# A build-time ordering that learns of a shared SBUF port: Nyström attention and two feed-forward layers on one core

## Chip, core and metric

The kernel runs on one core of one Trainium2 chip. The metric is the device time of one execution in microseconds (us), the median over runs.

## What is computed

The reference runs three stages one after another, all in float32. Cut to what matters:

```python
# attention: 4 batches, 8 heads, 576 tokens, head width 64, 32 landmarks
q_lm = q.reshape(B, H, 32, 18, D).mean(axis=3)      # landmark means: sums of 18 rows
k_lm = k.reshape(B, H, 32, 18, D).mean(axis=3)
A, Bm, C = sm(q, k_lm), sm(q_lm, k_lm), sm(q_lm, k)  # softmax, scale 1/8
Z = Bm.T / (norm_1 * norm_inf + 1e-6)
for _ in range(6):
    Z = 2 * Z - Z @ Bm @ Z
x = A @ Z @ C @ v                                    # then (2304, 512)
h = x @ w_in                                         # 512 -> 2048
x = (h * tanh(softplus(h))) @ w_out                  # 2048 -> 512
h = x @ moe2_w_in
out = (h * sigmoid(h)) @ moe2_w_out
```

## The kernel before

**The work.** Attention is done in eight groups, each of one batch and four heads (class `Group`). For a group the keys `kn` and queries `qn` come in, `sums` (line 739) forms the landmark sums `lmk` and `lmq`, `transposed` (763) turns keys and queries, `main` (801) forms the 32 by 32 middle matrix, `c_side` (931) and `a_side` (998) the two outer softmaxes, and `newton` (901) the six iterations. A group leaves a 64 by 128 block `ut` of a small matrix and its softmax `at`.

`projection` (523) multiplies a batch's `ut` with 512 columns of the first layer's input weights `wa`, which gives `wp`; it is called "the first projection" below for batch 0 and columns 0 to 511, "the second" for batch 0 and the next 512. From then on the layers run in units: a unit of phase 0 or 1 is a pair of products for 288 tokens and 128 hidden columns, `emit_h` (573), then the activation `z` on ScalarE (ACT), its rounded copy and remainder `g` (`gated`, 592), and `emit_o` (610). Phase 0 takes the first half of the hidden columns of the first layer, and stores its sums to DRAM in `yh`; phase 1 takes the second half and adds what `partial` (636) reads back from `yh`; phase 2 is the second layer. Each product is made of three passes with numbers split in a rounded part and a remainder. Weights are stored as 64-bit numbers; `decode` (421) turns them into float32 on ACT and VectorE (DVE, tile `m` or `wa`) and splits them with a copy and a subtraction.

**The order.** The order of all instructions is set while the program is built, by `Line`: a table of how long each engine takes (`cost`), when each tile was last written or read (`depend`), and when each engine comes free. A step of the program that is due goes next on its engine; an operation that two engines can do goes to the one that `issue` (163) expects to end first: landmark sums to VectorE or GpSimd (POOL) (line 744), copies to ACT or VectorE, subtractions to VectorE or GpSimd. On the chip each engine then runs its list in that order and waits on semaphores. The estimate has therefore no part in the run; it only decides which instruction stands where, and on which engine.

**Padding.** While groups are unfinished, the loop writes two transposes of the identity matrix, with no use for their result, wherever TensorE is free by the estimate and has done little lately:

```python
            if not grown and line.cold():
                for ring in (y_r, h_r, t_r):
                    if ring.idle(line.now):
                        b_ = ring.take([128, 512], FP32)
                        for i in range(2):
                            T.transpose(out=b_[0][:, i * 128:i * 128 + 128], in_=ident, identity=ident)
```

In lists and rows they read `y<-ident`, `h<-ident` or `t<-ident`. They are instructions like others: TensorE does them in their place in the list. All instructions of `issue` have one line in a profile (193 before), so rows are told apart by tile names. PE is TensorE, PEld its weight loads, SP the engine that issues all transfers.

Of the kernel before, what the change touches and what calls it, by code (L numbers as in the profile page):

```python
# [52 lines left out]
def width(ap):  # L53
    return ap.size() // ap.shape[0]


class Line:
# [12 lines left out]
    def __init__(self, nc):  # L70
        self.nc = {"V": nc.vector, "A": nc.scalar, "P": nc.gpsimd, "T": nc.tensor}
        self.free = dict.fromkeys(["V", "A", "P", "T", "D", "W"], 0.0)
        self.now = 0.0
        self.free["D"] = 0.45
        self.end = 0.0
        self.last = set()
        self.past = collections.deque()
        self.busy, self.seen = {}, {}
        self.chains = []
        self.small = False  # L80
        self.count = itertools.count()

    def cost(self, e, name, kw):
        src = kw.get("in_", kw.get("in0"))
        n = width(src if name == "tensor_reduce" else kw["out"])
        psum = src is not None and src.space == bass.MemoryType.PSUM
        more = 0.0
        if e == "T":
            tiled = kw["out"].shape[0] < 96 and "lhsT" in kw
            if tiled and (kw["out"].start_partition() or kw["lhsT"].start_partition()):  # L90
                return 0.027 * self.clock()
            n *= self.clock() * self.columns(kw)
        elif e == "A":
            more = -0.04 if psum else 0.0
            more += 0.14 if "accum_out" in kw else 0.09 if kw.get("func") == ACTF.Ln else 0.0
        elif e == "P" and name == "tensor_scalar":
            n *= 0.46
        elif e == "V" and name in ("copy", "tensor_copy", "tensor_scalar", "scaled"):
            if not psum:
                n *= 0.5  # L100
            elif n < 300:
                n += 50
            more = 0.06 if hasattr(kw.get("scalar1"), "space") else 0.0
        elif e == "V" and name == "reciprocal" and n > 1:
            more = 0.09
        return self.FIXED[e] + more + n * self.EACH[e]

    @staticmethod
# [48 lines left out]
    def lately(self):  # L157
# [2 lines left out]
            self.past.popleft()  # L160
        return sum(x[1] for x in self.past)

    def issue(self, engines, name, kw, bias=0.0):
        def start(e):
            return max(self.now, self.free[e], self.depend(e, name, kw))

        e = min(engines, key=lambda e: start(e) + self.cost(e, name, kw) + (bias if e == "V" else 0.0))
        at = start(e)
        if e == "T":
            small = kw["out"].shape[0] < 96  # L170
            if self.small and not small:
                at = max(at, self.free["T"] + 0.055)
            self.small = small
        end = at + self.cost(e, name, kw)
        if e == "T":
            tick = int(at / self.WINDOW)
            rows = kw["lhsT" if "lhsT" in kw else "in_"].shape[0]
            part = rows * kw["out"].shape[0] / 16384 * self.columns(kw)
            self.past.append((at, width(kw["out"]) * part))
            self.busy[tick] = self.busy.get(tick, 0) + width(kw["out"]) * part  # L180
        self.free[e] = end
        self.end = max(self.end, end)
        self.last.add(e)
        self.record(e, kw, end)
        if name == "copy" and e != "A":
            name = "tensor_copy"
        if name == "scaled":
            k = dict(out=kw["out"], in_=kw["in_"])
            if e == "A":
                name, kw = "activation", dict(k, func=ACTF.Copy, scale=kw["scalar1"])  # L190
            else:
                name, kw = "tensor_scalar", dict(out=kw["out"], in0=kw["in_"], scalar1=kw["scalar1"], scalar2=None, op0=ALU.mult)
        r = getattr(self.nc[e], name)(**kw)  # L193
        return r
# [57 lines left out]
class Ring:  # L252
# [11 lines left out]
    def any(self):  # L264
        return any(p[1] for p in self.pools)
# [37 lines left out]
def kernel(  # L303
# [29 lines left out]
    NB = {0: 2 * B, 1: 2 * B, 2: -(-NT // 512)}  # L333
# [3 lines left out]
    def tokens(ph, t):  # L337
        return (t * SH, SH) if ph < 2 else (t * 512, min(512, NT - t * 512))
# [3 lines left out]
    V, A, P, T = (On(line, e) for e in "VAPT")  # L342
# [48 lines left out]
    def until(cond):  # L391
        while not cond():
            yield "W"

    def marked(*m):
        return lambda: all(a in marks for a in m)
# [239 lines left out]
    def partial(t):  # L636

        yp_t[t] = []
        n0, n = tokens(1, t)
        for d in range(KD):  # L640
            yield from until(lambda: ysb_r.any() and stored.get(("part", 0, t), LATE) <= line.now)
            yp_t[t].append(ysb_r.take([128, 512], FP32))
            line.transfer(nc.sync, out=yp_t[t][d][0][:, :n], in_=yh[d * 128:(d + 1) * 128, n0:n0 + n])
            yield "W"
# [456 lines left out]
    while todo or flight:  # L1101
# [52 lines left out]
        if hs:  # L1154
            line.add(gated(ph, t, f), "G", "A", line.free["T"] + 0.17 + SLACK)
            if first and ph == 1:
                line.add(partial(t), "C")
            if ph < 2 and t % 2 and f % 4 == 3:
                Ring.give(wp_t[t // 2, f // 4])
            if ph == 2 and last:  # L1160
                for x in x_t[t]:
                    Ring.give(x)
        else:
            Ring.give(g_t.pop((ph, t, f)))
            if ph < 2 and t == NB[ph] - 1:
                marks.add(("last", f))
# [33 lines left out]
```

## Time and profile before

| | |
|---|---|
| median of 3 runs | 891.68 us (890.7 to 892.5) |
| the profiled execution | 885.96 us |
| its span, first to last instruction | 884.1 us |
| busy: PE | 842.2 us (95%) |
| busy: PEld | 710.9 us (80%) |
| busy: DVE | 330.6 us (37%) |
| busy: ACT | 369.4 us (42%) |
| busy: POOL | 314.0 us (36%) |

The span is the time between the first and the last instruction of the profiled execution; its own time is 1.86 us longer. Busy shares are averages over the whole span. VectorE has next to nothing to do in the last third, so its share says little of the first.

### The profile page before, as it was taken

The numbers are of one execution on the slowest core, as the hardware profiler recorded it, in microseconds if no ns is written. First come the engines' busy times: TensorE is split into PE (matmuls) and PEld (weight loads), VectorE is DVE, ScalarE is ACT, GpSimd is POOL, SyncE is SP. The second block draws the span as 40 slices with busy tenths as digits, with TensorE's granted clock in tenths as the row PEclk, the third lists the DMA queues.
The fourth block names the chain that finished last, engine by engine and source line by source line (L and its number), as shares of the span: only waits on it lengthen the run. The fifth ranks groups of instructions, "written<-read, shape, count | busy, mean of one in ns | idle before, by whom it ended". The sixth has DMA issues, their size and how long they took to land.

```text
span 884.1 us, 14991 instructions
## 1 busy us (share of the span) xinstructions
PE 842.2 (95%) x5974; PEld 710.9 (80%) x5974; DVE 330.6 (37%) x618; ACT 369.4 (42%) x784; POOL 314.0 (36%) x310
## 2 busy tenths in 40 slices
PE   7789898989999999999999998999999999999996
PEld 5566576768989888999998886788888888888895
DVE  7989664544686572120108888300000000000000
ACT  4475666663555452433325444421232123212321
POOL 1343353222446372523326645521232123212221
PEclk9999999999999999999999999999999999999999
DMA  9665424100542531322226820020002000100100
GB/s 235 177 200 153 151 64 111 43 19 12 194 145 77 183 89 54 91 73 92 69 86 233 304 96 1 14 82 0 1 17 68 0 1 25 36 0 1 29 20 25
DMA packets 41861, 72.27 MB, mean 82 GB/s; under 512 B 5184, under 2 KB 29248, under 8 KB 41792
## 3 DMA queue, kind: packets, MB, share of 16 engines
q1 hardware_dynamic: 41792, 71.32, 26.7%
q8 instruction: 47, 0.77, 0.4%
q14 instruction: 22, 0.18, 0.1%
HBM read 57.15 MB, written 14.16 MB: 81 GB/s over the span
## 4 chain that ended last, share of the span: by engine, by line
PE 70%; DVE 13%; ACT 6%; DMA 5%; issue 3%; SPq 2%; POOL 0%; DVEq 0%; ACTq 0%; POOLq 0%
PE y L193 38%; PE h L193 28%; DVE m L193 7%; PE t L193 5%; DMA wst<-in_moe_w_out_dram 2%; ACT L193 2%; SPq L204 2%; DVE wa L193 1%; ACT z L193 1%; DMA kn<-in_k_dram 1%; ACT m L193 1%; DMA wst<-in_moe_w_in_dram 1%; ACT g L193 1%; DMA wp<-in_q_dram 1%; DVE lmk L193 1%
## 5 line engine op out<-in xcount | busy, mean ns | idle before, releaser
L193 POOL TENSOR_TENSOR g<-z,g 128x288 fp32r<-128x288 f32 (+2 forms) x196 | 198.8, 1021 | 379.8 <-ACT g L193 320.1
L193 PE MATMUL y<-g,wo 128*128 128x288 f32 x1536 | 229.2, 300 | 0.3 <-ACT ysb L193 0.3
L193 PEld LDWEIGHTS y<-g,wo 128*128 128x128 f32 x1536 | 209.2, 188 | 14.4 <-issue 10.8
L193 ACT ACTIVATE z<-h 128x288 f32<-128x288 f32 (+2 forms) x208 | 96.2, 468 | 284.7 <-PE h L193 252.5
L193 PE MATMUL h<-x,wi 128*128 128x512 f32 (+1 forms) x960 | 205.8, 371 | 2.6 <-DVE wi L193 1.8
L193 PE MATMUL y<-wo,g 128*128 128x512 f32 x864 | 203.1, 392 | 0.6 <-POOL g L193 0.6
L193 PEld LDWEIGHTS h<-x,wi 128*128 128x128 f32 x960 | 167.6, 188 | 36.9 <-DVE wi L193 1.7
L193 PEld LDWEIGHTS y<-wo,g 128*128 128x128 f32 x864 | 161.8, 188 | 36.6 <-POOL g L193 1.0
L193 PE MATMUL h<-at,wp 128*128 128x288 f32 x768 | 122.1, 303 | 9.7 <-ACT z L193 9.5
L193 PEld LDWEIGHTS h<-at,wp 128*128 128x128 f32 x768 | 107.0, 189 | 21.9 <-ACT z L193 13.1
L193 ACT CAST g<-z 128x288 fp32r<-128x288 f32 (+2 forms) x199 | 96.0, 491 | 21.7 <-PE y L193 18.0
L193 DVE SCALAR_TENSOR_TENSOR m<-wst,m 128x512 int32<-128x512 int32 x96 | 97.3, 1014 | 2.7
L193 DVE TENSOR_TENSOR x<-xst,x 128x512 fp32r<-128x512 f32 (+1 forms) x4 | 4.3, 1066 | 181.5 <-ACT x L193 181.4
L193 POOL TENSOR_TENSOR wo<-m,wo 128x512 fp32r<-128x512 f32 x29 | 39.5, 1363 | 59.5 <-ACT wo L193 41.0
L193 DVE TENSOR_SCALAR m<-m 128x512 int32<-128x512 int32 x48 | 33.2, 692 | 26.3 <-ACT m L193 26.2
L193 DVE TENSOR_TENSOR wp<-t,wp 128x512 fp32r<-128x512 f32 x32 | 20.6, 685 | 43.5 <-ACT wp L193 43.5
L193 DVE TENSOR_TENSOR ysb<-y,ysb 128x288 f32<-128x288 f32 x32 | 13.2, 458 | 60.1 <-PE y L193 60.1
L193 ACT ACTIVATE m<-wst 128x512 f32<-128x512 f32 x48 | 31.8, 669 | 1.6 <-DMA wst<-in_moe_w_out_dram 1.1
L193 POOL TENSOR_TENSOR x<-xst,x 128x512 fp32r<-128x512 f32 (+1 forms) x16 | 19.3, 1209 | 33.7 <-ACT x L193 33.7
L193 ACT ACT_TABLE_LOAD x23 | 29.5, 1283 | 2.8 <-PE h L193 1.7
L193 ACT CAST wp<-t 128x512 fp32r<-128x512 f32 x29 | 15.6, 589 | 32.2 <-PE t L193 32.2
L193 ACT CAST wo<-m 128x512 fp32r<-128x512 f32 x20 | 12.4, 620 | 33.6 <-DVE m L193 33.6
(158 smaller groups left out, 573.5 us busy)
## 6 DMA issues: line engine op xcount, KB each, us to landing
wst<-in_moe_w_out_dram SPq DMA_DIRECT2D x32, 512.0 KB, 7.4
wst<-in_moe_w_in_dram SPq DMA_DIRECT2D x28, 512.0 KB, 6.3
kn<-in_k_dram SPq DMA_DIRECT2D x32, 144.0 KB, 7.4
vn<-in_v_dram SPq DMA_DIRECT2D x8, 576.0 KB, 6.8
yh<-ysb SPq DMA_DIRECT2D x32, 144.0 KB, 1.8
ysb<-yh SPq DMA_DIRECT2D x32, 144.0 KB, 2.3
ys<-ysb SPq DMA_DIRECT2D x32, 144.0 KB, 2.2
out_dram<-ysb SPq DMA_DIRECT2D x72, 64.0 KB, 1.7
```

The costliest lines, as they stand in the source:

```text
L193: r = getattr(self.nc[e], name)(**kw)
L204: return engine.dma_start(**kw)
```

## The change

Three things change. `cost` adds 0.9 us to a long reduction on VectorE, which are the landmark sums. [...] And `partial` waits until all of phase 0's sums are on their way to DRAM before it takes buffers.

```diff
@@ __init__
+        self.held = {"V": collections.deque(), "P": collections.deque()}
@@ cost
+        elif e == "V" and name == "tensor_reduce" and n > 1000:
+            more = 0.9
@@ new functions of Line
+    @staticmethod
+    def holds(e, name, kw):
+
+        if e == "P":
+            return True
+        src = [kw[k] for k in ("in_", "in0", "in1") if k in kw]
+        if e != "V" or any(x.space == bass.MemoryType.PSUM for x in src):
+            return False
+        return len(src) > 1 or name in ("copy", "tensor_copy", "tensor_scalar", "scaled")
+
+    def alone(self, e, at, name, kw):
+
+        if self.holds(e, name, kw):
+            for a, b in self.held["P" if e == "V" else "V"]:
+                if a < at + 0.05 and b > at:
+                    at = max(at, b)
+        return at
@@ issue
         def start(e):
-            return max(self.now, self.free[e], self.depend(e, name, kw))
+            at = max(self.now, self.free[e], self.depend(e, name, kw))
+            return self.alone(e, at, name, kw)
...
+        if self.holds(e, name, kw):
+            self.held[e].append((at, end))
+            while len(self.held[e]) > 24:
+                self.held[e].popleft()
@@ partial
+        yield from until(marked(("part", 0, NB[0] - 1)))
```

No operation is computed differently. What changes is the order, the engine of those operations that have a choice, and the padding. Over the whole program the lists differ in these counts:

| | before | now |
|---|---|---|
| padding transposes on TensorE | 214 | 312 |
| of them ahead of the first projection | 88 | 142 |
| of them ahead of the second projection | 190 | 264 |
| landmark sums on VectorE / on GpSimd | 10 / 6 | 8 / 8 |
| copies of `wo` and `wi` on VectorE / on ACT | 18 / 30 | 4 / 44 |
| subtractions of `wo` and `wi` on VectorE / on GpSimd | 8 / 40 | 1 / 47 |
| subtractions of `g` on VectorE / on GpSimd | 12 / 180 | 1 / 191 |
| table loads on ACT | 23 | 29 |

The three places below are those that the prediction speaks of. Instructions have line 193 before and 219 now.

TensorE, the third to the sixth iteration of `newton` for the first group (`t<-yu`; `h<-yu` is the second group's), before:

```order
L193 MATMUL t<-yu 32x96 x4
L193 MATMUL y<-ident 128x128 x8
L193 MATMUL h<-yu 32x96 x4
L193 MATMUL t<-yu 32x96 x4
L193 MATMUL y<-ident 128x128 x4
L193 MATMUL h<-yu 32x96 x4
L193 MATMUL t<-yu 32x96 x4
L193 MATMUL y<-ident 128x128 x4
L193 MATMUL h<-yu 32x96 x4
L193 MATMUL y<-ident 128x128 x4
L193 MATMUL t<-yu 32x64 x4
```

and now:

```order
L219 MATMUL t<-yu 32x96 x4
L219 MATMUL y<-ident 128x128 x16
L219 MATMUL h<-yu 32x96 x4
L219 MATMUL t<-yu 32x96 x4
L219 MATMUL y<-ident 128x128 x8
L219 MATMUL h<-yu 32x96 x4
L219 MATMUL t<-yu 32x96 x4
L219 MATMUL y<-ident 128x128 x6
L219 MATMUL h<-yu 32x96 x4
L219 MATMUL t<-yu 32x64 x4
```

Between the same iterations stand 30 padding transposes where there were 20.

TensorE around the first projection (`t<-wa,ut`), before:

```order
L193 MATMUL y<-ident 128x128 x4
L193 MATMUL t<-wa,ut_136 32x512 x8
L193 MATMUL y<-ident 128x128 x14
L193 MATMUL t<-lmT 32x32 x4
L193 MATMUL y<-ident 128x128 x6
L193 MATMUL h<-at_656,wp 128x288 x2
L193 MATMUL t<-Tk,lmT 32x288 x8
L193 MATMUL h<-at_656,wp 128x288 x16
```

and now:

```order
L219 MATMUL t<-lmT 32x32 x4
L219 MATMUL y<-ident 128x128 x10
L219 MATMUL t<-wa,ut_136 32x512 x8
L219 MATMUL y<-ident 128x128 x22
L219 MATMUL t<-Tk,lmT 32x288 x8
L219 MATMUL h<-at_632,wp 128x288 x18
```

The third group's small product `t<-lmT` moved ahead of the projection, its scores `t<-Tk,lmT` ahead of the first unit's products, and the padding behind the projection grew from 20 to 22 and that ahead of it from 4 to 10.

ACT, from the small softmax `eb` to the softmax `ec` of the sixth group, with the activations `z` and copies `g` of units between them, before:

```order
L193 ACT_TABLE_LOAD
L193 ACTIVATE eb,sbm<-t,nmb 128x32
L193 COPY ut_138<-t 64x128
L193 ACTIVATE bn<-eb,rb 128x32
L193 ACTIVATE ec,sc_2249<-t,nmc 128x288 x2
```

and now:

```order
L219 ACT_TABLE_LOAD
L219 ACTIVATE eb,sbm<-t,nmb 128x32
L219 CAST g<-z 128x288
L219 ACT_TABLE_LOAD
L219 ACTIVATE z<-h 128x288
L219 CAST g<-z 128x288
L219 ACTIVATE z<-h 128x288
L219 CAST at_2456<-a_t 128x576
L219 CAST g<-z 128x288
L219 ACT_TABLE_LOAD
L219 ACTIVATE ec,sc_2496<-t,nmc 128x288 x2
```

Between a group's two exponentials now stand activations of units, and with them two more table loads.

## Rows read from the trace of the kernel before

**Rows 1.** Stretches: length; busy us of PE, PEld, DVE, ACT, POOL; clock, DMA share, GB/s.

```profile
0.00:20.00 20.00, 14.87 (x141) 10.98 (x141) 13.45 (x33) 9.00 (x25) 1.52 (x13) 1.00 0.95 236
20.00:44.70 24.70, 19.08 (x313) 13.68 (x312) 24.60 (x64) 12.32 (x31) 9.51 (x9) 1.00 0.69 182
44.70:92.60 47.90, 43.79 (x525) 31.18 (x524) 43.34 (x105) 30.98 (x70) 18.72 (x19) 1.00 0.60 176
...
98.10:217.60 119.50, 109.39 (x1204) 86.06 (x1198) 59.56 (x168) 72.03 (x153) 39.92 (x47) 0.99 0.19 52
217.60:600.00 382.40, 372.77 (x2453) 336.08 (x2453) 182.76 (x231) 166.70 (x364) 170.93 (x158) 1.00 0.34 109
600.00:884.10 284.10, 276.83 (x1298) 230.29 (x1296) 2.02 (x2) 74.98 (x138) 72.11 (x64) 0.99 0.07 17
```

**Rows 2.** PE's waits, 20 to 100 us: total us, times, longest.

```profile
PE t L193 <- DVE yu L193: 4.7, 8, 1.1
PE t L193 <- ACT Tk L193: 2.0, 2, 1.6
PE h L193 <- DVE yu L193: 1.0, 1, 1.0
```

**Rows 3.** PE's waits, 100 to 215 us.

```profile
PE h L193 <- ACT z L193: 3.5, 4, 1.2
PE t L193 <- ACT ec L193: 3.0, 2, 1.9
PE t L193 <- ACT Tk L193: 1.3, 1, 1.3
```

**Rows 4.** PE's waits, 215 to 600 us.

```profile
PE h L193 <- ACT z L193: 6.0, 7, 1.2
```

**Rows 5.** Order of time on PE around padding: start us, us, operation.

```profile
45.88 1.75 PE L193 MATMUL y<-ident 128*128 128x128 f32 x14
47.56 0.27 PE L193 MATMUL t<-lmT 64*32 64x32 f32 x8
...
74.14 2.36 PE L193 MATMUL h<-ident 128*128 128x128 f32 x18
76.51 0.37 PE L193 MATMUL t<-yu 32*32 32x96 f32 x8
```

**Rows 6.** Order of time, all engines, 21 us: one VectorE shift beside GpSimd.

```profile
21.19 1.16 POOL L193 TENSOR_TENSOR at<-at,am 128x576 f32<-128x576 f32 x1 [18.84 <-DVE rc L193]
...
21.48 1.15 DVE L193 TENSOR_SCALAR wa<-wa 128x512 int32<-128x512 int32 x1
```

**Rows 7.** Tile wa, all its instructions: duration ns min/median/max.

```profile
L193 DVE TENSOR_SCALAR wa<-wa x16: 355/424/1295, 21.5 to 264.3; 128x512 int32<-128x512 int32 x16
```

**Rows 8.** Groups of instructions, 0 to 215 us: count, busy us, mean ns, idle before.

```profile
L193 DVE TENSOR_REDUCE lmk<-kn 128x64 f32<-128x1152 f32 x5 | 10.9, 2188 | 5.7 <-DMA kn<-in_k_dram 5.7
L193 DVE TENSOR_REDUCE lmq<-wp 128x64 f32<-128x1152 f32 x1 | 2.2, 2160 | 0.1
L193 POOL TENSOR_TENSOR t<-kn 128x576 f32<-128x576 f32 x3 | 4.9, 1642 | 0.0
L193 DVE CAST wo<-m 128x512 fp32r<-128x512 f32 x3 | 2.4, 790 | 0.0
L193 DVE TENSOR_TENSOR g<-z,g 128x288 fp32r<-128x288 f32 x5 | 3.4, 684 | 2.5 <-ACT g L193 1.9 <-POOL at L193 0.6
```

**Rows 9.** ACT's table loads, 0 to 215 us: count, busy us, mean ns.

```profile
L193 ACT ACT_TABLE_LOAD x22 | 28.2, 1283 | 2.8 <-PE h L193 1.7 <-PEq L1184 0.7
```

**Rows 10.** Order of time on ACT from 145 us.

```profile
145.33 1.28 ACT L193 ACT_TABLE_LOAD   x1
146.63 0.41 ACT L193 ACTIVATE z<-h 128x288 f32<-128x288 f32 x1
```

**Rows 11.** The same columns as rows 1, 100 to 120 us.

```profile
100.00:120.00 20.00, 16.66 (x190) 12.96 (x189) 11.69 (x23) 12.88 (x26) 8.36 (x10) 0.91 0.01 4
```

**Rows 12.** The page's costliest groups: the addition of the stored half product.

```profile
L193 DVE TENSOR_TENSOR ysb<-y,ysb 128x288 f32<-128x288 f32 x32 | 13.2, 458 | 60.1 <-PE y L193 60.1
```

## Prediction

> **What bounds the kernel now.** I began with busy time by stretch [rows 1], because the averages over the span hide the stages. From 600 us on TensorE is busy 276.8 of 284.1 us with the second layer's products, and from 217.6 to 600 us 372.8 of 382.4. The work there is fixed, so the change can win only what TensorE idles: 9.6 us in the middle. Before 217.6 us the eight groups run. VectorE is busy 24.6 of 24.7 us up to the first projection (44.7 us) and 43.3 of 47.9 up to the second (92.6 us): it sets the pace there, and TensorE idles 5.6 and 4.1 us although padding fills many holes. From 98.1 to 217.6 us VectorE is at half, TensorE at 109.4 of 119.5, so TensorE's own list sets the pace, with 10.1 us idle. In all, 29.4 us of TensorE idling between 20 and 600 us is what a better order could take back.
>
> Next I read who ends those waits. Up to 100 us it is mostly VectorE's Newton step `yu`, 4.7 and 1.0 us, then ACT with 2.0 [rows 2]. From 100 to 215 us it is ACT: 3.5 us for `z`, 3.0 for `ec`, 1.3 for `Tk` [rows 3]. Behind that it is ACT's `z` again, 6.0 us [rows 4]. Who waits for whom matters here, because the new estimate knows more of VectorE and GpSimd and nothing new of ACT.
>
> **The change, term by term.** The sum is made against the profiled execution, 885.96 us, which lies 5.7 us under the median of the runs shown; I add the same difference to both.
>
> *Padding.* 98 more transposes. A run of 14 took from 45.88 us to the next instruction at 47.56, 0.120 us each; a run of 18 took from 74.14 to 76.51, 0.132 each [rows 5]. 54 of the 98 stand ahead of the first projection (54 x 0.120 = 6.5 us), 20 between first and second (2.6), 24 behind (3.2): **+12.3 us** of TensorE time in its list. Padding costs nothing where TensorE would wait anyway; that is counted as a smaller idle time in the next terms, never twice. Bounds: 98 x 0.120 = 11.8 and 98 x 0.132 = 12.9.
>
> *Waits for VectorE.* Up to the last group's Newton step VectorE loses work: two landmark sums at 2.19 and 2.16 us, three copies of `wo` at 0.79 and four subtractions of `g` at 0.68 [rows 8], 9.4 us, and some smaller items. The sums go to GpSimd, whose first of five additions alone takes 1.64 us [rows 8], so a sum ends later there but no longer holds up the Newton steps behind it on VectorE. With less work and a TensorE that comes later because of the padding, VectorE should be ready first. Of the 5.7 us of waits for `yu` [rows 2] between none and all could go; I take 5.0, nearer all, since both effects push the same way: **-5.0 us**.
>
> The price of the port speaks against taking everything. GpSimd's subtraction ran from 21.19 for 1.16 us, and VectorE's shift of `wa`, started 0.29 us later, took 1.15 us and ended 0.28 us after it [rows 6]; the fastest of these shifts took 0.355 us, the slowest 1.295 [rows 7]. So the second waits for the first, as the new rule assumes. [...]
>
> *Waits for ACT behind 217.6 us.* ACT runs in order, and a weight copy that waits for VectorE's decode holds the `z` behind it. The new order knows that decode and GpSimd's subtractions block each other, and gives 14 of the weight copies of VectorE to ACT. Of the 6.0 us [rows 4] I take two thirds: **-4.0 us**; the ends are -6.0 and, since ACT gets the copies, +2.
>
> *Table loads.* ACT loads a table when it changes between the exponential and the activation. Six more stand in the list, between the groups' softmaxes. One takes 1.28 us [rows 10], and the 22 loads up to 215 us took 28.2 us [rows 9], so six are 7.7 us of ACT. TensorE's waits on ACT there are 2.0 + 3.5 + 3.0 + 1.3 = 9.8 us [rows 2, 3], 0.35 us for each us of load; that would make +2.7. I take half, because ACT has 40% of its time free from 98.1 to 217.6 us [rows 1]: **+1.4 us**, with ends 0 and 7.7. The row also shows the activation starting 0.02 us behind the load's end [rows 10]. [...]
>
> *Clock.* From 100 to 120 us the granted clock averaged 0.91 [rows 11], behind the longest waits; 0.09 x 20 = 1.8 us were lost. With more padding ahead half of that may come back: **-0.9 us** (ends 0 and -1.8).
>
> *The wait in `partial`.* It moves the loads of the half product behind phase 0's last store in SP's queue. Each feeds a VectorE addition, and these waited 60.1 us in all, every bit for the product on TensorE [rows 12], none for a transfer: **0**. Without that cover each load's landing would be paid once per tile. SP's list keeps its transfers; some weight loads move by a few places, ahead of stores, and no wait of TensorE above is for them. The tail and the second layer keep their lists but for a few engines: 0.
>
> Sum: 12.3 - 5.0 - 4.0 + 1.4 - 0.9 = **+3.8 us**. That is 889.8 us for a profiled execution, and **895.5 us** on the median. A difference under 0.2%, 1.8 us, can't be told from none.
>
> **Rivals.**
>
> *Padding fills holes that are there anyway (faster).* If the new estimate is close to the chip, every pair of transposes stands where TensorE would have waited, and the list moves on when VectorE does. Then the 5.7 us [rows 2], the 6.0 us [rows 4], the clock's 1.8 us and half of ACT's 7.8 us [rows 3] all go: 12.3 - 5.7 - 6.0 - 1.8 - 3.9 = -5.1 us, 886.6. It decides from the point where more than 12.3 of the 29.4 idle us go [rows 1]. For it speaks VectorE at over 90% up to 92.6 us; against it, that ACT, of which the estimate learns nothing, ends most waits from there on.
>
> *Balance (no change).* Idle time falls by as much as padding adds, within 1.8 us: 891.7. It needs two thirds of the waits for ACT to go as well.
>
> *Table loads on the path (clearly slower).* All six land between a group's two exponentials while TensorE waits for `ec` or `z`: 12.3 - 5.0 - 4.0 - 0.9 + 7.7 = +10.1, 901.8. The third place of the order shows two of them just there; ACT's free 40% speaks against all six.
>
> [...]
>
> That the change does nothing is ruled out by the lists: the padding alone differs by 98.
>
> **How the numbers follow.** Forecast (+1.8 to +9 us) 0.33; table loads 0.12; the port 0.10; balance 0.18; holes filled 0.27. So faster 0.27, same 0.18, slower 0.55. The range runs from the faster rival's 886 to 904, short of the last 0.5 us of the port's case; the likeliest case alone would be 893.5 to 901.
>
> **What would show it.** Right: PE's `ident` groups hold 312; the first projection starts near 47 us and the second near 96 (92.6 + 9.1 - 5.0 = 96.7); waits for `yu` up to 100 us fall under 1.5 us; 29 table loads, and waits for `ec` and `z` between 100 and 215 us stay at 6 us or more; VectorE's busy share ahead of the second projection falls. Wrong: the second projection starts at 92 us or earlier with TensorE idling under 3 us ahead of it, which is the faster rival; waits for `z` from 100 us on that double, which is the table loads; long shifts and copies on VectorE and waits for `yu` as before, which is the port.

## The result

The changed kernel takes **876.39 us** (876.36 to 877.22, 4 runs) against 891.83 us (890.7 to 892.5, 4 runs) for the kernel before: ratio 0.983, 95% interval 0.9813 to 0.9847, 15.4 us less. The prediction said 895.5 us, and its range began at 886: the sign was wrong, and the range too. The change ran a second time on another chip and gave 876.84 against 889.74 us there, ratio 0.9855 [0.9835, 0.9875].

The profiled execution took 876.36 us with a span of 874.6. That of before took 885.96 with 884.1, so the two profiles differ by 9.6 us and the medians by 15.4. The difference between these two differences is a subject of its own, the first of the experiments.

The page's first part, busy time of each engine after the change:

```profile
PE 851.0 (97%) x6072; PEld 720.7 (82%) x6072; DVE 300.2 (34%) x566; ACT 386.6 (44%) x814; POOL 348.4 (40%) x344
```

TensorE is busy 8.8 us more than the 842.2 us of before (98 transposes at 0.12 us would be 11.8, so its other work takes some 3 us less), and idles 23.6 us of the span where it idled 41.9. The busy time by stretch, the columns as in [rows 1], cut at the first projection (45.4 us), the second (85.6) and the eighth (219.2):

```profile
0.00:20.00 20.00, 15.97 (x152) 12.06 (x153) 8.93 (x24) 10.02 (x28) 9.42 (x24) 1.00 0.95 243
20.00:45.40 25.40, 24.09 (x365) 19.35 (x363) 25.40 (x72) 14.05 (x35) 9.05 (x9) 1.00 0.80 233
45.40:85.60 40.20, 38.94 (x469) 29.95 (x468) 35.16 (x89) 24.77 (x57) 17.39 (x16) 1.00 0.70 206
85.60:219.20 133.60, 126.69 (x1369) 96.78 (x1368) 61.21 (x173) 95.26 (x193) 51.40 (x61) 1.00 0.18 50
219.20:600.00 380.80, 376.67 (x2462) 338.96 (x2462) 166.91 (x206) 171.76 (x374) 188.91 (x171) 1.00 0.34 109
600.00:874.60 274.60, 268.60 (x1262) 223.59 (x1261) 2.62 (x5) 70.69 (x129) 72.24 (x65) 1.00 0.07 18
```

From 20 us to the second projection TensorE idles 1.3 + 1.3 us; it was 5.6 + 4.1 [rows 1]. From there to the eighth projection it is 6.9 us where 98.1 to 217.6 us alone had 10.1, behind that to 600 us 4.1 where it was 9.6, and in the rest 6.0 where it was 7.3. VectorE is still busy every microsecond from 20 us to the first projection, but only 35.2 of 40.2 us up to the second.

TensorE's waits after the change, 20 to 100 us (total us, times, longest); they answer to [rows 2]:

```profile
PE h L219 <- DVE yu L219: 0.9, 3, 0.5
PE t L219 <- ACT ec L219: 0.8, 1, 0.8
...
PE t L219 <- DVE yu L219: 0.3, 1, 0.3
```

The same view from 100 to 215 us, for [rows 3]:

```profile
PE t L219 <- ACT ec L219: 2.7, 4, 1.2
PE h L219 <- ACT z L219: 2.0, 3, 1.0
PE t L219 <- ACT Tq L219: 0.8, 1, 0.8
```

And from 215 to 600 us, for [rows 4]:

```profile
PE h L219 <- ACT z L219: 2.0, 2, 1.2
PE y L219 <- POOL g L219: 1.1, 2, 0.9
PE h L219 <- POOL wi L219: 0.6, 2, 0.4
```

The waits for `yu` fell from 5.7 to 1.2 us, those for `ec` and `z` from 6.5 to 4.7, and the `z` behind the groups from 6.0 to 2.0.

Two groups of TensorE's instructions in the first 100 us of the kernel before, the units' products:

```profile
L193 PE MATMUL y<-g,wo 128*128 128x288 f32 x48 | 10.0, 322 | 0.0
L193 PE MATMUL h<-at,wp 128*128 128x288 f32 x38 | 6.1, 307 | 0.0
```

And after the change:

```profile
L219 PE MATMUL y<-g,wo 128*128 128x288 f32 x61 | 10.8, 310 | 0.0
L219 PE MATMUL h<-at,wp 128*128 128x288 f32 x48 | 8.6, 312 | 0.3 <-ACT z L219 0.3
```

In the same 100 us TensorE now does 23 more products (109 against 86) and 74 more padding transposes (282 against 208), and VectorE has done 24 Newton steps (`yu<-yu`) where it was 23. More of everything fits because less time goes in waiting. At the eighth projection 566 products are done, at 219.21 us, where it was 540 at 217.57: it comes 1.6 us later with 26 products more behind it. The first projection came at 45.42 us (44.69 before), the second at 85.62 (92.62). The second is no like-for-like mark, though: 19 Newton steps on VectorE stand ahead of it and 21 did before, so part of its 7 us is a projection moved ahead of a group's work.

Where the 9.6 us lie can be read from three marks. From the start of the eighth projection to that of the 1,934th of the 2,304 products it took 204.6 us for 1,394 products before and takes 195.3 for 1,368, 0.147 and 0.143 us each. The 26 products done ahead are worth 3.8 us, less the 1.6 us of lateness: 2.2 us. The faster pace is worth 1,368 x 0.004 = 5.5 us. What comes after that product is 1.8 us shorter. Together 9.5 us of the 9.6.

### The profile page after: what moved, and what is told of

Its sections match the earlier page's. It is cut to its first block, busy times and chain, and to the rows that moved or that the text cites. A ratio compares the mean times of both kernels' runs of the same rounds, so it can differ in the third digit from the quotient of the medians.

```text
span 874.6 us, 15200 instructions
## 1 busy us (share of the span) xinstructions
PE 851.0 (97%) x6072; PEld 720.7 (82%) x6072; DVE 300.2 (34%) x566; ACT 386.6 (44%) x814; POOL 348.4 (40%) x344
## 5 line engine op out<-in xcount | busy, mean ns | idle before, releaser
L219 POOL TENSOR_TENSOR g<-z,g 128x288 fp32r<-128x288 f32 (+2 forms) x207 | 205.0, 998 | 376.2 <-ACT g L219 304.7
L219 ACT CAST g<-z 128x288 fp32r<-128x288 f32 (+2 forms) x206 | 99.1, 488 | 15.9 <-PE y L219 12.1
L219 DVE SCALAR_TENSOR_TENSOR m<-wst,m 128x512 int32<-128x512 int32 x96 | 99.2, 1051 | 1.3
L219 POOL TENSOR_TENSOR wo<-m,wo 128x512 fp32r<-128x512 f32 x31 | 46.4, 1497 | 38.0 <-ACT wo L219 38.0
L219 DVE CAST x<-xst 128x512 fp32r<-128x512 f32 (+1 forms) x4 | 2.9, 721 | 160.8 <-PE h L219 160.8
L219 POOL TENSOR_TENSOR x<-xst,x 128x512 fp32r<-128x512 f32 (+1 forms) x20 | 24.7, 1233 | 36.0 <-ACT x L219 35.2
L219 POOL TENSOR_TENSOR wi<-m,wi 128x512 fp32r<-128x512 f32 x16 | 24.3, 1516 | 11.1 <-ACT wi L219 11.0
```

## The experiments

The theory after the result: padding stands almost wholly where TensorE would have waited, so it was wrong to charge it; the gain comes from an order in which VectorE and GpSimd deliver when the list says so, partly ahead of the groups' end and partly behind it. Rivals: the gain comes from one small part of the change alone (the price of the sums, or the wait in `partial`); it comes from the padding itself, if that keeps TensorE's granted clock up (a mean of 0.996 in the profile of before, 0.999 after); or it is the luck of one list among many. Ratios are against the kernel before on the same chip.

"The port's rule" below is `holds` with `alone`: in the estimate, an operation that `holds` names begins only when those of the other engine have ended. The trace of the kernel before shows such waiting between VectorE's shifts and GpSimd's operations. Of 96 shifts `m<-wst,m`, 42 ran beside no operation of GpSimd and took 0.66 to 0.69 us, 54 beside one or more and took 0.68 to 1.79. Of the 41 that began within one, 40 ended 0.55 to 0.65 us after its end. GpSimd's subtractions of `wo` and `wi` took 1.27 to 1.30 us with no shift of `m` or `wa` beside them and 1.29 to 1.76 with one or more. That a shared port is the cause is the author's reading; no row shows it.

### How far the kernel before spreads by itself

No edit: the kernel before, run again.

> The kernel before, unchanged, against itself. The change took 9.6 us off the profiled execution (885.96 to 876.36) but 15.4 us off the median (891.83 to 876.39), so 5.8 us are open. Theory A: the kernel before has executions of several lengths, because its idle stretches sometimes let the clock fall; then single times here spread over 885 to 893 us and the profile shows a granted clock under that of the changed kernel (0.999). Theory B: the two figures come from different conditions and the kernel is steady; then all times lie within 1 us of each other.

Measured: 890.11 us (888.28 to 893.26, 12 runs) against 890.61 (887.56 to 893.64, 23 runs), ratio 0.9998 [0.9986, 1.001]. Runs of the same list lie up to 6 us apart; the eight runs of the changed kernel lie between 876.36 and 878.01. That is Theory A. The profiled execution of this run has a span of 889.3 us and a mean granted clock of 0.982, that of before had 884.1 and 0.996. Two stretches of it, and a piece of the first (columns as in [rows 1]):

```profile
100.00:110.00 10.00, 7.36 (x46) 5.75 (x46) 3.85 (x15) 7.74 (x16) 2.89 (x3) 0.69 0.07 29
...
104.00:105.00 1.00, 0.38 (x9) 0.20 (x8) 0.94 (x6) 0.99 (x1) 0.00 (x0) 0.50 0.00 0
...
150.00:160.00 10.00, 7.49 (x72) 4.64 (x70) 3.18 (x10) 8.43 (x17) 4.27 (x5) 0.75 0.50 118
```

The first and the last of these in the profile that the prediction was made on:

```profile
100.00:110.00 10.00, 7.67 (x62) 5.61 (x62) 2.99 (x11) 6.92 (x16) 3.71 (x4) 0.83 0.02 6
...
150.00:160.00 10.00, 8.83 (x94) 6.73 (x92) 4.78 (x20) 7.55 (x18) 3.69 (x5) 1.00 0.48 120
```

The list is the same, yet TensorE does 94 matmuls from 150 to 160 us in one execution and 72 in the other, at a clock of 1.00 and 0.75, and the eighth projection starts at 217.57 and at 222.50 us. What TensorE did around the fall of its clock, from 101 us on in this run, in order of time (start us, us, operation, and in brackets its idle time before and who ended it):

```profile
101.35 0.79 PE L193 MATMUL h<-at,wp 128*128 128x288 f32 x4 [0.44 <-ACT z L193]
103.26 0.31 PE L193 MATMUL t<-yu 32*32 32x64 f32 x8 [1.11 <-ACT ec L193]
...
105.46 0.85 PE L193 MATMUL h<-at,wp 128*128 128x288 f32 x2 [1.09 <-ACT z L193]
```

From 104 us the granted clock is 0.50, and from 111 us it is back at 1.00. The first two waits stand ahead of the fall, the third lies in the slow stretch. So waits of 0.44 and 1.11 us for `z` and `ec` are followed here by a stretch at 0.50; that they bring it about is the author's reading, which no run tests by itself. The changed kernel's profile stays at 1.00 in every stretch up to 600 us. The 5.8 us by which the medians differ more than the profiles are about this: this execution of the list before, 1 us above its median, is 5.2 us longer than the one that the sum was made on.

### The wait in `partial` alone

```diff
+        yield from until(marked(("part", 0, NB[0] - 1)))
```

> The kernel before with the new wait in partial alone. The prediction's term is 0: 889 to 892 us, same as before within 0.2%. A cost of the moved loads would show as waits of VectorE's addition on a transfer.

Measured: 890.44 us (887.09 to 893.86), ratio 1.0 [0.9981, 1.0018]. That term was 0 and is 0.

### The price of the sums alone, and the port's rule alone

The first kernel has only the new price in `cost`:

```diff
+        elif e == "V" and name == "tensor_reduce" and n > 1000:
+            more = 0.9
```

> The kernel before with the new price of the landmark sums alone (242 padding transposes, 23 table loads). With the port rule alone at -4.6 us: if both parts simply add up, the price is worth the other 10 us, 880 to 882 us. If they only work together, 886 to 891 us.

Measured: 899.37 us (896.01 to 902.93), ratio 1.0102 [1.0074, 1.0129], **9.6 us slower** than the kernel before. The first line of TensorE's waits from 20 to 100 us, and the second projection in order of time:

```profile
PE t L195 <- DVE yu L195: 6.8, 6, 2.2
...
101.99 1.09 PE L195 MATMUL t<-wa,ut 64*32 64x512 f32 x16
```

The time is above both ranges of the expectation. Sums go to GpSimd as they do in the changed kernel, eight and eight, but without the rule the estimate reckons with no delay of VectorE beside them. Whether such a delay is what costs the time can be looked for in VectorE's shifts of `wa`, two kinds, in the first 102 us (count, busy us, mean ns). This kernel:

```profile
L195 DVE SCALAR_TENSOR_TENSOR wa<-aw,wa 128x512 int32<-128x512 int32 x8 | 7.4, 919 | 0.0
L195 DVE SCALAR_TENSOR_TENSOR wa<-wst,wa 128x512 int32<-128x512 int32 x8 | 5.8, 720 | 0.0
```

The changed one:

```profile
L219 DVE SCALAR_TENSOR_TENSOR wa<-aw,wa 128x512 int32<-128x512 int32 x8 | 5.3, 680 | 0.0
L219 DVE SCALAR_TENSOR_TENSOR wa<-wst,wa 128x512 int32<-128x512 int32 x8 | 7.3, 919 | 0.0
```

One kind is longer here, the other in the changed kernel; together they are busy 13.2 us here, 12.6 there and 12.0 in the kernel before. So longer shifts are not what makes this kernel late. From the first projection to the second VectorE is idle 11.7 of 54.2 us, where it was 4.6 of 47.9 [rows 1], and TensorE's granted clock averages 0.94 (columns as in [rows 1]):

```profile
47.80:102.00 54.20, 45.49 (x506) 32.91 (x506) 42.48 (x105) 31.04 (x67) 18.75 (x20) 0.94 0.50 145
```

VectorE's longest waits from 20 to 102 us are for ACT:

```profile
DVE asm L195 <- ACT at L195: 4.5, 2, 3.6
DVE scm L195 <- ACT ec L195: 3.4, 1, 3.4
```

The waits for `yu` grow, and the second projection is 9.4 us later than in [rows 1], with VectorE waiting for others more than before. The time lies towards the end of the prediction's range, as its case of the port does, but one sign of that case, long shifts and copies on VectorE, is not in the rows; why ACT delivers late in this list stays open. In the trace of the kernel before, a sum on VectorE that ran beside GpSimd's additions for 2.09 us (from 82.39 us) took 2.21 us, one beside none (from 10.70 us) 2.16. What it costs to move a sum to GpSimd no run here shows by itself.

The second kernel is the changed one without those two lines.

> The port rule without the new price of the landmark sums: 270 padding transposes in place of 312 and 23 table loads in place of 29. Theory A (the port does it): 877 to 880 us, TensorE's waits for yu up to 100 us under 2 us. Theory B (the price of the sums matters as much): 883 us or more, with waits for yu of 4 us or more.

Measured: 886.06 us (882.78 to 888.63), ratio 0.9952 [0.9934, 0.997], 4.6 us faster; TensorE does 270 padding transposes there and ACT loads 23 tables. The time is Theory B's, although the waits for `yu` up to 100 us are only 0.5 us, Theory A's sign: they are not what decides here. TensorE's waits for ACT from 100 to 217 us:

```profile
PE h L217 <- ACT z L217: 4.3, 3, 2.3
PE t L217 <- ACT ec L217: 3.3, 3, 2.0
```

So neither part alone makes the gain in these lists. One costs 9.6 us, the other saves 4.6, and both together save 13 to 15: the price is worth 8 to 11 us once the rule is there. Each is a single list, though, and lists made with the same knowledge lie up to 10 us apart (the last experiment), so these sizes are not those of the parts to a few microseconds.

### The new estimate only ahead of the groups' end, and only behind it

`know` switches the rule off (first kernel) or on (second) when the last group is done; in the second the sums keep their old price, too. The first:

```diff
+    def know(self):
+        return not self.late
...
-        if self.holds(e, name, kw):
+        if self.know() and self.holds(e, name, kw):
...
             grown = 1
+            line.late = True
```

> The new rule and the new price hold only until the eight groups are done; from then on the list is made by the old estimate. Theory A (both stages gain): TensorE's idle time up to the groups' end stays at 13 to 14 us as in the changed kernel, and ACT's z makes it wait some 6 us behind it again: 879 to 882 us. Theory B (the whole gain is in the groups' stage): 876 to 877 us.

Measured: 887.58 us (885.22 to 889.61), ratio 0.9968 [0.9955, 0.9982], 3.0 us faster, less than both theories said. Up to the groups' end its list is that of the changed kernel. TensorE's waits from 217 to 600 us:

```profile
PE h L223 <- ACT z L223: 6.3, 6, 1.8
PE h L223 <- DVE wi L223: 3.9, 3, 2.1
```

The second kernel has `return self.late` in `know`, and the price under `and self.late`.

> The reverse: the old estimate until the groups are done, the new rule behind. The groups' stage is word for word that of the kernel before, so its 25 us of TensorE idling must come back. Theory A: the waits for z behind 217 us fall from 6.0 to about 2 us and 5 to 7 us are won: 884 to 887 us on the median. Theory B: nothing is won, 891 us.

Measured: 883.4 us (881.43 to 885.28), ratio 0.9921 [0.9909, 0.9933], 7.2 us faster, with 214 padding transposes and the list of before up to the groups' end. That is 0.6 us under Theory A's range, with somewhat more waiting for `z` than it said. The same view of its waits:

```profile
PE h L223 <- ACT z L223: 3.2, 5, 1.1
PE y L223 <- POOL g L223: 1.6, 1, 1.6
```

About half of the gain is behind the groups, where no padding changes and no sum is left. What changes there is shown by ACT's part in the decode, the conversion `m<-wst` and the copies behind it, from 215 to 600 us (count, busy us, mean ns, idle before and who ended it), before:

```profile
L193 ACT ACTIVATE m<-wst 128x512 f32<-128x512 f32 x40 | 26.4, 667 | 1.0 <-DMA wst<-in_moe_w_out_dram 0.5 <-POOL g L193 0.4
L193 ACT CAST wo<-m 128x512 fp32r<-128x512 f32 x15 | 9.3, 620 | 32.4 <-DVE m L193 32.4
L193 ACT CAST wi<-m 128x512 fp32r<-128x512 f32 x10 | 6.2, 621 | 19.9 <-DVE m L193 19.9
```

and after:

```profile
L219 ACT ACTIVATE m<-wst 128x512 f32<-128x512 f32 x40 | 26.9, 675 | 27.8 <-POOL wi L219 12.2 <-POOL wo L219 11.6 <-DMA wst<-in_moe_w_in_dram 3.7
L219 ACT CAST wo<-m 128x512 fp32r<-128x512 f32 x22 | 13.6, 617 | 5.8 <-DVE m L219 5.8
L219 ACT CAST wi<-m 128x512 fp32r<-128x512 f32 x14 | 8.6, 618 | 1.5 <-DVE m L219 1.5
```

ACT stood 52.3 us in front of these copies waiting for VectorE's decode, with activations behind them in its list. Now it does 36 copies instead of 25 and stands 7.3 us in front of them. Part of the waiting moved to the step ahead, which waits 27.8 us, mostly until GpSimd has done with the tile, where it waited 1.0; in all ACT stands 35.1 us there and stood 53.3. The decode itself is not faster: VectorE's shifts `m<-wst,m` take 1,106 ns on average there after the change and took 1,056 before. The rule does not keep the two engines off each other; it makes the estimate know when a shift will end, and the copy stands in ACT's list where its input is nearly ready.

A rival is that it is enough to move copies to ACT. Two lists of the last experiment, both with its number `SLACK` at 0.27, speak against it. The kernel before:

```profile
L193 ACT CAST wo<-m 128x512 fp32r<-128x512 f32 x21 | 13.0, 621 | 38.9 <-DVE m L193 38.9
L193 ACT CAST wi<-m 128x512 fp32r<-128x512 f32 x11 | 6.8, 621 | 17.9 <-DVE m L193 17.8
```

The changed kernel:

```profile
L219 ACT CAST wo<-m 128x512 fp32r<-128x512 f32 x23 | 14.2, 617 | 4.3 <-DVE m L219 4.3
L219 ACT CAST wi<-m 128x512 fp32r<-128x512 f32 x14 | 8.6, 613 | 2.6 <-DVE m L219 2.6
```

Without the rule ACT does 32 of these copies, nearly as many as the change's 36, and still stands 56.8 us in front of them; with it, 37 copies and 6.9 us.

The two savings add up to 10.2 us, the whole to 13 to 15. Where they lie can be read at the start of the eighth projection, in one trace of each kernel:

| | eighth projection starts | products done by then | time behind it |
|---|---|---|---|
| kernel before, profile of the prediction | 217.6 | 540 | 666.5 |
| kernel before, run again | 222.5 | 540 | 666.8 |
| price of the sums alone | 231.6 | 566 | 668.8 |
| port's rule alone | 224.6 | 540 | 660.0 |
| new estimate only ahead | 219.6 | 566 | 666.3 |
| new estimate only behind | 221.8 | 540 | 660.3 |
| the whole change | 219.2 | 566 | 655.4 |

Where as many products were done, the rule makes the time behind 6 to 7 us shorter (660.0 and 660.3). The changed groups' stage leaves 26 products fewer to do, at 0.147 us each 3.8 us, but under the old estimate the rest takes as long as before with them gone. Only both together keep this gain, which is about what the two savings lack.

### Padding

Three kernels, none of which touches a result: padding has no use for its output. In the first, the kernel before does a third transpose for each pair, 107 more (321 in all), with the order otherwise unchanged:

```diff
+                        nc.tensor.transpose(out=b_[0][:, 256:384], in_=ident, identity=ident)
```

> The list of the kernel before, with a third transpose behind each padding pair: 321 in place of 214, nothing else moved. Theory P (padding is paid in full, as the prediction's first term has it): 107 x 0.125 = +13 us, 903 to 905 us. Theory H (padding fills holes, and the work behind it arrives no later; what it adds is a clock that does not fall): between -4 and +5 us, 886 to 895 us, with a mean granted clock over 0.995.

Measured: 892.36 us (890.22 to 895.74) against 889.98, ratio 1.0027 [1.0012, 1.0043], **2.4 us for 107 transposes, 0.022 us each**. That is Theory H in time but not in the clock: its mean over the profile is 0.988, not over 0.995. The second projection comes at 96.11 us, 2.6 us after the 93.55 of the run without an edit.

In the second, the changed kernel leaves out every third pair behind the first six (212 are left of 312), with the estimate and so the order as they were:

```diff
+                        line.mute = line.pads > 6 and line.pads % 3 == 0
                         for i in range(2):
                             T.transpose(out=b_[0][:, i * 128:i * 128 + 128], in_=ident, identity=ident)
+                        line.mute = False
```

> The list of the changed kernel with every third padding pair left out behind the first six: 212 transposes in place of 312, as many as before; all other instructions in the changed order. Theory P: 100 x 0.125 = 12 us less, 863 to 866 us. Theory H: TensorE waits in place of the padding, and the clock falls in some stretches: 875 to 881 us. Either way it shows what the new order of the other instructions is worth without the added padding, against 890.6.

Measured: 874.99 us (874.86 to 876.11), ratio 0.9829 [0.9814, 0.9844]; the whole change had 0.983 and 0.9855. By medians, on different chips, that is 1.4 to 1.9 us less for 100 transposes, by ratios 0 to 2.3. At 0.125 us each they are 12.5 us of TensorE's time. Theory H is right again but for the clock, which did not fall. TensorE's waits from 20 to 100 us show what took their place; for `yu` it now waits 4.3 us, after the change 1.2:

```profile
PE t L223 <- DVE yu L223: 2.3, 4, 1.0
PE h L223 <- DVE yu L223: 2.0, 3, 0.9
```

The third keeps only the first 12 transposes.

> The changed kernel's list with 12 padding transposes in place of 312. Theory P: 300 x 0.125 = 37 us less, 840 us. Theory H: the groups' stage takes about as long, and the granted clock is at its lower level for much of it: 885 us or more, mean clock under 0.95.

Measured: 879.72 us (878.22 to 880.54), ratio 0.9878 [0.9861, 0.9894], about 3 us slower than the change and 4.7 slower than with 212 transposes on the same chip. It lies between the theories, nearer H, and the mean clock of its profile is 0.974, where H had under 0.95. From 20 to 100 us in both (columns as in [rows 1]), every third pair left out first:

```profile
20.00:100.00 80.00, 70.22 (x922) 50.50 (x904) 70.94 (x184) 49.75 (x116) 37.02 (x36) 1.00 0.61 179
```

```profile
20.00:100.00 80.00, 57.01 (x698) 36.92 (x696) 69.04 (x178) 45.69 (x108) 35.01 (x35) 0.72 0.61 179
```

With 12 transposes TensorE is busy 57.0 of 80 us and its granted clock averages 0.72 over the stretch; with 212 it is 1.00. Even so the second projection is only 2.3 us later than in the changed kernel (87.94 against 85.62 us): TensorE idles 23.0 of the 80 us even so, where it idles 9.8 with 212, so it waits for others, slow or not. So padding is worth 3 to 5 us as a whole here, and a third more or less of it next to nothing. The rival that the gain is made by the extra padding falls: the change keeps all of its gain with a third fewer, and the kernel before gets none from a half more.

### Table loads, and ACT's and GpSimd's fixed times

The prediction noted that the estimate learns nothing of ACT. In this kernel `cost` adds 1.3 us where the activation function differs from the one before on ACT:

```diff
+            more += 1.3 if self.other(kw) else 0.0
...
+    def other(self, kw):
+        return kw.get("func") in (ACTF.Exp, ACTF.Mish, ACTF.Silu) and kw["func"] != self.table
...
+        if e == "A" and self.other(kw):
+            self.table = kw["func"]
```

> The changed kernel, whose estimate also learns that ACT pays 1.3 us when it changes between the exponential and the two layer activations. 302 padding transposes, 27 table loads. Theory A (ACT's waits between 100 and 215 us are what is left of a wrong estimate): waits for ec and z there fall from 4.7 to under 2.5 us, and 872 to 875 us. Theory B: the list is only as good as before, the groups end later behind a more cautious estimate: 876 to 882 us.

Measured: **867.22 us** (866.45 to 868.31), ratio 0.974 [0.9724, 0.9755], some 9 us less than the change and less than either theory said. TensorE's waits for ACT from 100 to 217 us:

```profile
PE t L226 <- ACT ec L226: 1.7, 3, 0.8
PE h L226 <- ACT z L226: 1.1, 1, 1.1
```

They are 2.8 us, after the change 4.7, before 6.5. The number of loads hardly falls, from 29 to 27; what falls is the waiting for them. TensorE idles 19.6 of the span's 866.0 us (23.6 after the change) and is busy 846.4 (851.0); where those 4.6 busy us went was not followed further than to ten padding transposes fewer. The eighth projection comes at 213.4 us, 5.8 us earlier than after the change, with 588 products done instead of 566, 3.2 us at 0.147: the whole gain lies ahead of it.

On top of it, the fixed times of ACT (0.1 to 0.17 us) and GpSimd (0.05 to 0.1) were raised:

```diff
-    FIXED = {"V": 0.07, "A": 0.1, "P": 0.05, "T": 0.0133}
+    FIXED = {"V": 0.07, "A": 0.17, "P": 0.1, "T": 0.0133}
```

> The kernel with table loads known (867.2 us), whose estimate also gets 0.07 us more for each ACT and 0.05 us more for each GpSimd operation, as their rows show (ACT 0.41 us for 288 elements, GpSimd 0.80). If a closer estimate goes on paying: 862 to 866 us. If what is left is the work itself: 866 to 870 us; TensorE idles only 20 of 866 us in that kernel.

Measured: 866.24 us (865.97 to 866.29), ratio 0.9733 [0.9714, 0.9752]. That is the fastest of all, 23.5 us under the kernel before, but 1 us from the last one is within what lists differ by, as the next runs show, and it falls between the two ranges: whether a closer estimate goes on paying is not decided. On its chip the changed kernel was run again:

> The changed kernel again, on one chip with the next three, so that they can be compared. 876 to 877 us; its times should lie within 1.5 us of each other, since its clock hardly falls, while the kernel before spreads over 5 us and more.

Measured: 876.84 us (876.52 to 878.01), the ratio 0.9855 given at the top.

### Is it the luck of one list?

`SLACK` is a number of the order that the change does not touch, 0.30. Moving it gives other lists with the same knowledge.

```diff
-SLACK = 0.3
+SLACK = 0.27
```

> The kernel before, with the estimate's margin SLACK at 0.27 in place of 0.30, a number that has nothing to do with ports: many places of the list move, no reason is added. If the change's 13 to 15 us are the rule's, these neighbours of the kernel before stay within 5 us of it (885 to 895 us). If they are a lucky list, neighbours scatter as widely as the change moved: over 10 us.

> The kernel before with SLACK at 0.33. Rule: 885 to 895 us. Luck: more than 10 us away from 890.

> The changed kernel with SLACK at 0.27. Rule: 872 to 882 us, faster than both neighbours of the kernel before. Luck: 883 us or more.

> The changed kernel with SLACK at 0.33. Rule: 872 to 882 us. Luck: 883 us or more.

Measured, against 891.2 us (887.38 to 894.15, 18 runs) for the kernel before on this chip:

| `SLACK` | kernel before | changed kernel |
|---|---|---|
| 0.27 | 887.22, ratio 0.9962 [0.9945, 0.9979] | 872.36, ratio 0.9793 [0.9778, 0.9808] |
| 0.30 | 891.2 | not run on this chip: ratio 0.983, 0.9855 elsewhere |
| 0.33 | 890.23, ratio 0.9995 [0.9981, 1.001] | 882.92, ratio 0.9915 [0.9898, 0.9931] |

The old lists stay within 4 us of each other, and the worst of the changed lists (882.92) is faster than the best of the old ones (887.22), so the knowledge counts. But the gain is 14.9 us at 0.27 and 7.3 at 0.33: a list of the changed kind lies some 5 us to either side of its middle, and by that half of the 15 us at 0.30 could be luck. The last run is at the border that its expectation set. The traces tell the lasting part from the other. At 0.27 the changed kernel's eighth projection starts at 215.8 us with 560 products done and 655.8 us behind it, and that of before at 219.3 with 554 and 666.1; at 0.33 it is 215.0, 542 and 663.8 against 218.7, 554 and 671.0. With 0.147 us for each product done more or fewer, the time behind is 9.5 and 9.0 us shorter in these pairs and 7 to 8 in that at 0.30. So the saving behind the groups comes back in every pair. What varies is how many products the groups' stage gets done: 6 more at 0.27, 26 more at 0.30, 12 fewer at 0.33. Why is open; the number of table loads does not order them (25, 29 and 21).

## Why the prediction was wrong

- **The step that failed is "Padding: 98 more transposes, +12.3 us".** It charged every transpose in full and left it to the next terms to give back what falls into waits, although it had itself read that VectorE sets the pace up to the second projection. Measured, 107 more in the list of before cost 2.4 us, and 100 fewer in the new list save about 2 at most: 0.02 us each, a sixth of the 0.125 charged. The rows said so: VectorE was busy 43.3 of 47.9 us up to the second projection [rows 1], and only 24 of the 98 stand behind it. Padding is written by the estimate where it expects TensorE to wait; when VectorE sets the pace it is an effect of waiting and not a cost. TensorE's busy time did grow, by 8.8 us, but where the terms for waits gave back 7.6 us net (5.0 + 4.0 - 1.4), its idle time fell by 18.3.
- **"Waits for VectorE: -5.0 us"** is right by its own row (5.7 to 1.2 us, so -4.5), and too narrow as a sum. TensorE's idle time up to the eighth projection fell from 24.9 us (5.1 up to 20 us, then 5.6, 4.1 and 10.1) to 13.5, 11.4 us in all. The row of one releaser is no bound for what an order can take back; the stage's whole idle time is.
- **"Waits for ACT behind 217.6 us: -4.0 us"** was right in place and mechanism: 6.0 to 2.0 us, copies on ACT from 25 to 36 there, the late kernel alone 7.2 us faster. That the size fits to the tenth is luck: with the new estimate only behind it, the same wait is 3.2 us. All idle time there fell by 5.5 us.
- **"Table loads: +1.4 us"** had the wrong sign as a net: 29 loads as foretold, but the waits for `ec` and `z` are 4.7 us instead of 6.5, where 6 or more were foretold. They are no loss against before, but they are still paid: the list whose estimate knows them is 9 us faster. The rows show a load of 1.28 us and the activation 0.02 us behind its end [rows 10], and the 1.3 us that follows the rows was enough for that gain.
- **"Clock: -0.9 us"** was undersized. The sum was made against an execution with one dip [rows 11]; the one of the first experiment has several (0.69 from 100 to 110 us and 0.75 from 150 to 160, among others) and is 5.2 us longer, and the changed kernel's profiles have none up to 600 us. That the profile lay 5.7 us under the median was in front of me, and I added the difference to both sides as if it were fixed. It belonged to the kernel before alone.
- **"`partial`: 0"** was right, by a run of its own.

Of the rivals, "Padding fills holes that are there anyway" was the right one. It gave -5.1 us against the profile, where -9.6 came, since it still added the 12.3 us and took away four single rows instead of the idle time. The case of the port did not come: waits for `yu` up to 100 us are 1.2 us and not as before. The price without the rule is slow enough for it (899.37 us), but not by longer shifts. Of the signs named ahead, 312 transposes, 29 loads and waits for `yu` under 1.5 us up to 100 us came as foretold for the forecast; waits for `ec` and `z` of 6 us or more did not. The second projection at 85.6 us, with 1.3 us of idling ahead of it, was the sign named for the faster rival, though some of it is the order: two Newton steps fewer stand ahead.

## What to carry to other kernels

Ask of filler instructions which engine sets the pace where they stand: next to one that is busy some 90% of the time they cost a fraction of their length here (0.02 of 0.125 us each), and the bound for a better order is the idle time of the stage, not the wait of one releaser. One better number in a planner is not a better plan: the price of the sums alone lost 9.6 us, and with the port's rule the two gained 13 to 15. Judge it on several lists made with slightly other settings, since lists with the same knowledge lay 10 us apart here. Where the profiled execution lies outside the spread of the runs, look for what differs between executions of one program before adding the gap to both sides.

## What was not expected of the hardware

- The granted clock differs between executions of one program: 0.69 and 0.83 from 100 to 110 us, 0.75 and 1.00 from 150 to 160 us, with the same instructions in the same order; the slower execution is 5.2 us longer.
- A TensorE with its clock at 0.72 on average over 80 us of the kernel goes with only 3 us more of 876, in the run that also leaves out 300 padding transposes: it waits for other engines there.
- The shifts that the port's rule is about did not get shorter in the faster kernel. VectorE's `m<-wst,m` behind the groups took 1,106 ns instead of 1,056 on average, while the same shift takes 0.68 us elsewhere in the changed kernel (from 76.85 us); what fell is the time that others stand waiting for them.
